# Retention and a squared-ReLU feed-forward on one core: the state's two products in 64-column halves of the array

## The chip, the cores and the metric

One NeuronCore of a Trainium2 chip runs the whole kernel. Its engines are called as in the profile: PE is TensorE (matmuls), PEld its weight loads, DVE is VectorE, ACT is ScalarE, POOL is GpSimd, SP is SyncE, which issues the loads. The metric is the device time of one execution in microseconds (us), lower is better; several executions are timed and their median is given.

## The reference

Retention for 8 sequences of 576 positions and 8 heads of 64, then a feed-forward part over the 4608 tokens that come out (512 wide, 2048 inside):

```python
scores = scale * np.matmul(q, k.transpose(0, 1, 3, 2))
gamma = 1.0 - 2.0 ** (-5.0 - np.arange(H, dtype=np.float32))
Dmat = np.where(rel >= 0, gamma[:, None, None] ** rel[None, :, :], 0.0)   # rel = t - s
x = np.matmul(scores * Dmat[None], v)        # (B, H, S, D), then to (B*S, H*D)
h = np.maximum(x @ w_in, 0.0)
out = (h * h @ w_out).astype(np.float32)
```

q, k, v are float32. The two weights come as float64 and are rounded to float32 on the chip.

## The kernel before

A sequence is taken in chunks of 128 rows, so five of them: four of 128 rows and a last one of 64. With gamma^(t-s) written as gamma^t times gamma^-s, the output of a chunk is q' times a running state U, plus the masked scores of the chunk itself times v', where U is the sum of k^T v' over the chunks before. Heads are taken in pairs, since two heads of 64 fill the 128 partitions; `HP` = 4 is the number of pairs, `hp` counts them, and `e` is 0 or 1 within a pair.

A chunk goes through three functions:

- `turn` (L172) transposes q and k on TensorE (L178) and takes them out of PSUM, q on VectorE with its decay (L181), k on ScalarE (L183).
- `scores` (L185) makes the chunk's own scores (L193). A head's 64 dimensions lie on half of the partitions, so the two heads of a pair use the two row halves of the array. VectorE masks the scores into `ret` (L198) and scales v into `vs` (L202).
- `retain` (L205) makes x of the chunk, transposed, in one PSUM tile `x_ps`, and adds the chunk to U. For each pair the state's product comes first (L212): U of the pair lies in `u_sb` as a 128 x 128 block with one head's 64 x 64 on each end of the diagonal and zeros elsewhere, and one matmul over the whole array serves both heads. Then come the products with the masked scores (L215), one for each head, 64 output columns each, which land on partitions 0 to 63 and 64 to 127: the two column halves of the array. ScalarE copies x to `xT` (L225). U's growth (L231) is one matmul for each pair over the whole array: 128 columns of k against 128 of vs, of which only the two diagonal 64 x 64 blocks are used. ScalarE copies these two blocks of all pairs to the other of two `u_sb` buffers (L237). The first chunk of a sequence has no state's product, the last adds nothing to U.

The form that the profile gives a matmul, such as 128\*64, says how many rows and columns of the array it uses: the contraction by the output's partitions.

The feed-forward part takes blocks of 512 tokens: `ffn_in` (L243) makes 128 of the 2048 inner values for a block with four matmuls (L248), ScalarE applies ReLU (L251), VectorE squares (L253). `ffn_out` (L255) makes a quarter of the sum over the 2048 for 128 tokens with four matmuls (L262); VectorE copies the whole sum out (L266), and POOL's queue stores it (L268).

The order is written out by hand in the loop at L287: step i runs `retain` of chunk i - 2, `scores` of chunk i - 1 and `turn` of chunk i, and after each of the three a third of a chunk's share of feed-forward steps (`ffn`, L276), so that TensorE has work while results leave PSUM. Each step of the feed-forward part also prepares one of 32 pieces of the weights (`prepare`, L132), whose rounding is five operations on VectorE (L122, L127 to L130) and two on POOL (L123, L125), until all are ready. Every engine runs its instructions in the order in which they are written.

Of the kernel before, what the change touches and what calls it, by code (L numbers as in the profile page):

```python
# [9 lines left out]
F32 = mybir.dt.float32  # L10
# [1 line left out]
AF = mybir.ActivationFunctionType  # L12
ALU = mybir.AluOpType

C = 128  # rows of a sequence that are taken at once
TOK = 512  # tokens of a block of the feed-forward part
N_LD = 4  # chunks of q, k and v on chip at once


@with_exitstack  # L20
def kernel(
# [8 lines left out]
    decay_v: bass.AP,  # L30
    out: bass.AP,
):
    """Retention by chunks, with gamma^(t-s) as gamma^t * gamma^-s.

    q is scaled by gamma^t / sqrt(D) where its transpose leaves PSUM, v by gamma^-s, so that

        x[t] = sum_{s <= t} (q'[t] . k[s]) v'[s] = q'[t] U + (the same sum within t's chunk)

    with U = sum k[s]^T v'[s] over the chunks before, which accumulates in PSUM. x comes out
    transposed, as the first product of the feed-forward part takes it, and stays on chip.  # L40

    Everything is in float32. Weights that come in as float64 come as their bits, in int64,
    and are rounded to float32 here.
    """
    nc = tc.nc
    ctx.enter_context(tc.manual_schedule())

    B, H, S, D = q.shape
    HP = H // 2  # pairs of heads: a pair fills the 128 partitions
    d_model = H * D  # L50
    n_tok = B * S
    d_ff = moe_w_in.shape[1]
# [4 lines left out]
    NCH = -(-S // C)  # L57
    chunks = [(b, ci, ci * C, min(C, S - ci * C)) for b in range(B) for ci in range(NCH)]
    N_CH = len(chunks)
    N_PART = 4  # of the sum over d_ff  # L60

    const = ctx.enter_context(tc.tile_pool(name="const", bufs=1))
    ld = ctx.enter_context(tc.tile_pool(name="ld", bufs=N_LD))
    work = ctx.enter_context(tc.tile_pool(name="work", bufs=2))
# [7 lines left out]
    ps_u = ctx.enter_context(tc.tile_pool(name="ps_u", bufs=1, space=PS))  # L72
    ps_f = ctx.enter_context(tc.tile_pool(name="ps_f", bufs=2, space=PS))

    loaded = {}
# [7 lines left out]
            loaded[i].append(t)  # L83

    def w_tile(j):
        """Piece j of the weights: 128 of d_ff, of w_in first."""
        m = j % N_DF
        if j < N_DF:
            t = const.tile([128, N_DM, 128], F32, name=f"w_in{m}")
            src = moe_w_in.rearrange("(c p) f -> p c f", p=128)[:, :, m * 128:(m + 1) * 128]  # L90
        else:
            t = const.tile([128, N_DM, d_model // N_DM], F32, name=f"w_out{m}")
            src = moe_w_out[m * 128:(m + 1) * 128, :].rearrange("p (c f) -> p c f", c=N_DM)
        return t, src
# [13 lines left out]
        raws.append(raw)  # L108

    def round_w(j):  # L110
        """float64 bits to the nearest float32: (mantissa) * 2^(exponent), and the sign.

        What lies under float32's normal numbers becomes 0, what lies over them inf.
        """
        if raws[j] is None:
            return
        words = raws[j].rearrange("p c f -> p (c f)").bitcast(U32).rearrange("p (n two) -> p n two", two=2)
        lo, hi = words[:, :, 0], words[:, :, 1]
        t = w[j].rearrange("p c f -> p (c f)")
        bits = t.bitcast(U32)  # L120
        exp = exp_pool.tile([128, N_DM * 128], U32, tag="exp", name="exp")
        nc.vector.tensor_scalar(exp, hi, 20, 0x7FF, op0=ALU.logical_shift_right, op1=ALU.bitwise_and)  # L122
        nc.gpsimd.tensor_scalar(exp, exp, 1151.0, 896.0, op0=ALU.min, op1=ALU.max)  # L123
        # the bits of 2^(exponent - 1023)
        nc.gpsimd.tensor_scalar(exp, exp, -896.0, 2.0 ** 23, op0=ALU.add, op1=ALU.mult)  # L125
        # the mantissa's upper 21 bits, with the leading 1, and its lower 32 as a fraction
        nc.vector.tensor_scalar(bits, hi, 0xFFFFF, 0x100000, op0=ALU.bitwise_and, op1=ALU.bitwise_or)  # L127
        nc.vector.scalar_tensor_tensor(t, lo, 2.0 ** -32, bits, op0=ALU.mult, op1=ALU.add)
        nc.vector.scalar_tensor_tensor(t, t, 2.0 ** -20, exp.bitcast(F32), op0=ALU.mult, op1=ALU.mult)  # L129
        nc.vector.scalar_tensor_tensor(bits, hi, 0x80000000, bits, op0=ALU.bitwise_and, op1=ALU.bitwise_or)  # L130

    def prepare(last):  # L132
        """The next piece of the weights up to `last`; the loads run two ahead."""
        j = n_ready[0]
        if j > last:
            return
        if j + 2 < 2 * N_DF:
            fetch_w(j + 2)
        round_w(j)
        n_ready[0] += 1  # L140
# [12 lines left out]

    ident = const.tile([128, 128], F32, name="ident")
    make_identity(nc, ident)
    # 1 where t >= s, with s on the partitions
    msk = const.tile([128, 1, C], F32, name="msk")
    nc.gpsimd.memset(msk, 1.0)
    nc.gpsimd.affine_select(
        out=msk[:, 0, :], in_=msk[:, 0, :], compare_op=ALU.is_ge, fill=0.0, base=0,  # L160
        pattern=[[1, C]], channel_multiplier=-1,
    )
    # U of a pair of heads on the diagonal of a 128 x 128 block; the rest stays 0
    u_sb = [const.tile([128, HP, 128], F32, name=f"u_sb{j}") for j in range(2)]
    for t in u_sb:
        nc.gpsimd.memset(t, 0.0)
# [3 lines left out]
    u_ps = [None]  # L170

    def turn(i):  # L172
        """q' and k with the head's dimension on the partitions, two heads to a column block."""
        cs, c0 = chunks[i][3], chunks[i][2]
        for j, name in enumerate(("qT", "kT")):
            p = ps_a.tile([128, HP, C], F32, tag="a", name=f"{name}_ps")
            for hp in range(HP):
                nc.tensor.transpose(p[:, hp, :cs], loaded[i][j][:cs, 2 * hp:2 * hp + 2, :], ident[:cs, :cs])  # L178
            t = st[i][name] = work.tile([128, HP, C], F32, tag=name, name=name)
            if j == 0:  # L180
                nc.vector.tensor_tensor(t[:, :, :cs], p[:, :, :cs], dq[:, :, c0:c0 + cs], op=ALU.mult)  # L181
            else:
                nc.scalar.copy(t[:, :, :cs], p[:, :, :cs])  # L183

    def scores(i):  # L185
        """The chunk's own scores, [s, t], masked; the heads of a pair in banks of their own."""
        b, ci, c0, cs = chunks[i]
        qT, kT = st[i]["qT"], st[i]["kT"]
        sc = [ps_a.tile([128, HP, C], F32, tag="a", name=f"sc{e}") for e in range(2)]
# [13 lines left out]
                                dv[:cs, :, ci:ci + 1].to_broadcast([cs, H, D]), op=ALU.mult)  # L203

    def retain(i):  # L205
        """The chunk's x, transposed, and U with the chunk added."""
        b, ci, c0, cs = chunks[i]
        s = st[i]
        p = ps_a.tile([128, HP, C], F32, tag="a", name="x_ps")
        for hp in range(HP):  # L210
            if ci > 0:
                nc.tensor.matmul(p[:, hp, :cs], lhsT=u_sb[ci % 2][:, hp, :], rhs=s["qT"][:, hp, :cs],  # L212
                                 start=True, stop=False, skip_group_check=True)
            for e in range(2):
                nc.tensor.matmul(p[D * e:D * e + D, hp, :cs], lhsT=s["vs"][:cs, 2 * hp + e, :],  # L215
                                 rhs=s["ret"][e][:cs, hp, :cs], start=(ci == 0), stop=True,
                                 skip_group_check=True)
        tok = b * S + c0
        at = tok
        while at < tok + cs:  # L220
            n = at // TOK
            end = min(tok + cs, (n + 1) * TOK)
            if n not in xT:
                xT[n] = x_pool.tile([128, N_DM, TOK], F32, tag="xT", name="xT")
            nc.scalar.copy(xT[n][:, :, at - n * TOK:end - n * TOK], p[:, :, at - tok:end - tok])  # L225
            at = end
        if ci + 1 < NCH:
            if ci == 0:
                u_ps[0] = ps_u.tile([128, HP, 128], F32, tag="u", name="u_ps")
            for hp in range(HP):  # L230
                nc.tensor.matmul(u_ps[0][:, hp, :], lhsT=loaded[i][1][:cs, 2 * hp:2 * hp + 2, :],  # L231
                                 rhs=s["vs"][:cs, 2 * hp:2 * hp + 2, :], start=(ci == 0 and hp == 0),
                                 stop=(hp == HP - 1), skip_group_check=True)
            u = u_sb[(ci + 1) % 2]
            for e in range(2):
                sl = slice(D * e, D * e + D)
                nc.scalar.copy(u[sl, :, sl], u_ps[0][sl, :, sl])  # L237
        st[i] = loaded[i] = None

    g = {}  # L240
    acc = {}

    def ffn_in(n, m):  # L243
        """relu(x w_in)^2, transposed: 128 of d_ff by a block's tokens."""
        assert m < n_ready[0]
        p = ps_f.tile([128, TOK], F32, tag="h", name="h_ps")
        for cc in range(N_DM):
# [5 lines left out]
        nc.vector.tensor_tensor(g[n, m], r, r, op=ALU.mult)  # L253

    def ffn_out(n, ts, part):  # L255
        """A part of the sum over d_ff for 128 tokens of the block."""
        if part == 0:
            acc[0] = ps_f.tile([128, d_model], F32, tag="o", name="o_ps")
        end = (part + 1) * N_DF // N_PART
# [7 lines left out]
            row = n * TOK + ts * 128  # L267
            nc.gpsimd.dma_start(out[row:row + 128, :], o)  # L268

    # Steps of the feed-forward part stand between those of the retention, so that the tensor  # L270
    # engine has work while results leave PSUM. A block's steps last while as many tokens come in.
    steps = []
    owed = [0.0]
    PER_TOK = (N_DF + N_TS * N_PART) / TOK
# [35 lines left out]


def _decays(B, H, S, D):
    """gamma^t / sqrt(D) by [head's dimension in a pair, pair, t]; gamma^-s by [s in its chunk, head, chunk]."""
    import numpy as np

    gamma = 1.0 - 2.0 ** (-5.0 - np.arange(H))
    t = np.arange(S)
# [38 lines left out]
```

## Time and profile before

| | |
|---|---|
| runs, median | 1265.71 us (1264.05 to 1266.25, three runs) |
| profiled execution, its span | 1263.9 us, 10515 instructions |
| TensorE busy | 1222.0 us, 97% of the span |
| VectorE, ScalarE, POOL busy | 313.0, 154.4, 74.9 us |
| the feed-forward products L248 and L262 | 509.4 and 506.7 us of TensorE's time |
| the retention's products L193, L212, L215, L231 | 44.5, 60.3, 65.0, 39.2 us |
| granted clock of TensorE, mean | 0.986 |

The span runs from the first to the last instruction of the profiled execution; the page shows nothing of that execution outside its span. A group's line gives the source line, engine, operation, tiles and count, then busy time and mean nanoseconds of one, then the idle time of the engine ahead of them and what ended it. A float32 matmul shows as two records with a weight load each, so counts are twice the number of matmuls. Matmuls are pipelined and their ends are modelled, so the mean length of one is much longer than the distance between two; distances between starts are safer.

### The profile page before, as it was taken

What the parts mean: (1) busy time and instruction counts of PE and PEld (TensorE: products, weight loads), DVE (VectorE), ACT (ScalarE), POOL (GpSimd) and SP (SyncE); (2) the same over time, 40 slices, a digit from 0 to 9 for tenths busy, and PEclk for the clock granted to TensorE, in tenths of its full rate; (3) what the DMA queues carried; (4) which work ended last, traced back from release to release, by engine and by line L of the source; (5) the groups of instructions that cost most, each with busy time, mean ns of one, the idle gap of its engine ahead of it and who ended that gap; (6) DMA issues with size and microseconds to landing.
All of it is one profiled execution on the core that took longest, in us unless ns stands there. A gap on an engine that the chain in (4) does not pass through costs nothing.

```text
span 1263.9 us, 10515 instructions
## 1 busy us (share of the span) xinstructions
PE 1222.0 (97%) x4416; PEld 609.8 (48%) x4416; DVE 313.0 (25%) x500; ACT 154.4 (12%) x293; POOL 74.9 (6%) x110
## 2 busy tenths in 40 slices
PE   3698999999999999999999999999999999999998
PEld 2454544544445554445544554454544544444443
DVE  4888811221122112221112112211221122101200
ACT  1111100210012001110121001100210012000100
POOL 2333300000000000000000000000000000000000
PEclk9698999999999999999999999999999999999999
DMA  9655412001210112001110111101121000000000
GB/s 237 180 142 154 117 42 59 5 17 42 59 30 17 33 30 46 21 25 34 42 34 13 34 42 26 42 21 33 25 50 30 26 9 1 9 17 8 1 9 25
DMA packets 126479, 56.41 MB, mean 45 GB/s; under 512 B 113760, under 2 KB 121952, under 8 KB 126304
## 3 DMA queue, kind: packets, MB, share of 16 engines
q1 hardware_dynamic: 123552, 46.30, 15.9%
q0 software_dynamic: 2880, 9.44, 1.9%
q8 instruction: 35, 0.57, 0.2%
q14 instruction: 12, 0.10, 0.0%
HBM read 46.29 MB, written 9.44 MB: 44 GB/s over the span
## 4 chain that ended last, share of the span: by engine, by line
issue 72%; PE 18%; POOL 4%; DVE 4%; SPq 1%; DMA 0%; POOLq 0%
PE o_ps L262 8%; PE h_ps L248 7%; POOL exp L125 1%; POOL out_dram L268 1%; SPq L82 1%; POOL exp L123 1%; PE x_ps L215 1%; DVE w_in L129 1%; DVE w_in L130 1%; PE x_ps L212 1%; PE sc L193 1%; PE u_ps L231 1%; DVE exp L122 1%; DMA raw<-in_moe_w_in_dram 0%; DVE ret L198 0%
## 5 line engine op out<-in xcount | busy, mean ns | idle before, releaser
L248 PE MATMUL h_ps<-xT,w_in 128*128 128x512 f32 x1152 | 509.4, 596 | 0.0
L262 PE MATMUL o_ps<-w_out,g 128*128 128x512 f32 x1152 | 506.7, 594 | 0.0
L248 PEld LDWEIGHTS h_ps<-xT,w_in 128*128 128x128 f32 x1152 | 215.3, 191 | 253.0 <-issue 250.5
L262 PEld LDWEIGHTS o_ps<-w_out,g 128*128 128x128 f32 x1152 | 214.8, 190 | 253.5 <-issue 249.7
L253 DVE TENSOR_TENSOR g<-r 128x512 f32<-128x512 f32 x144 | 99.5, 691 | 405.6 <-ACT r L251 405.6
L251 ACT ACTIVATE r<-h_ps 128x512 f32<-128x512 f32 x144 | 86.0, 597 | 512.4 <-PE h_ps L248 487.5
L198 DVE TENSOR_TENSOR ret<-sc,msk 128x512 f32<-128x512 f32 (+1 forms) x80 | 47.0, 629 | 213.8 <-PE sc L193 213.8
L268 POOL DMA_DIRECT2D out_dram<-o_sb x36 | 19.6, 545 | 1084.0 <-DVE o_sb L266 1084.0
L266 DVE COPY o_sb<-o_ps 128x512 f32<-128x512 f32 x36 | 24.9, 692 | 202.1 <-PE o_ps L262 202.1
L215 PE MATMUL x_ps<-ret,vs 128*64 128x128 f32 (+1 forms) x640 | 65.0, 296 | 0.2 <-DVE vs L202 0.2
L212 PE MATMUL x_ps<-qT,u_sb 128*128 128x128 f32 (+1 forms) x256 | 60.3, 319 | 0.2 <-DVE ret L198 0.2
L212 PEld LDWEIGHTS x_ps<-qT,u_sb 128*128 128x128 f32 x256 | 42.4, 197 | 29.4 <-issue 27.8
L183 ACT COPY kT<-kT_ps 128x512 f32<-128x512 f32 (+1 forms) x40 | 21.7, 543 | 282.7 <-PE kT_ps L178 282.4
L193 PEld LDWEIGHTS sc<-qT,kT 64*128 64x128 f32 (+1 forms) x640 | 37.1, 183 | 32.1 <-issue 30.9
L225 ACT COPY xT<-x_ps 128x512 f32<-128x512 f32 (+1 forms) x44 | 22.0, 509 | 235.2 <-PE x_ps L215 235.2
L178 PE MATMUL kT_ps<-ident,k_ld 128*128 128x128 f32 (+1 forms) x160 | 25.1, 283 | 26.5 <-DVE ret L198 26.4
L181 DVE TENSOR_TENSOR qT<-qT_ps,dq 128x512 f32<-128x512 f32 (+1 forms) x40 | 25.3, 633 | 100.5 <-PE qT_ps L178 90.5
L193 PE MATMUL sc<-qT,kT 64*128 64x128 f32 (+1 forms) x640 | 44.5, 280 | 5.2 <-DVE qT L181 5.2
L215 PEld LDWEIGHTS x_ps<-ret,vs 128*64 128x64 f32 (+1 forms) x640 | 33.8, 141 | 20.7 <-issue 6.9
L231 PE MATMUL u_ps<-vs,k_ld 128*128 128x128 f32 x256 | 39.2, 299 | 0.0
L231 PEld LDWEIGHTS u_ps<-vs,k_ld 128*128 128x128 f32 x256 | 33.0, 201 | 6.0 <-issue 6.0
L178 PEld LDWEIGHTS kT_ps<-ident,k_ld 128*128 128x128 f32 (+1 forms) x160 | 18.8, 149 | 28.2 <-DVE ret L198 27.7
(25 smaller groups left out, 253.3 us busy)
## 6 DMA issues: line engine op xcount, KB each, us to landing
out_dram<-o_sb POOLq DMA_DIRECT2D x36, 256.0 KB, 2.3
q_ld<-in_q_dram SPq DMA_DIRECT2D x32, 256.0 KB, 4.5
k_ld<-in_k_dram SPq DMA_DIRECT2D x32, 256.0 KB, 3.3
v_ld<-in_v_dram SPq DMA_DIRECT2D x32, 256.0 KB, 4.1
raw<-in_moe_w_in_dram SPq DMA_DIRECT2D x16, 512.0 KB, 4.4
raw<-in_moe_w_out_dram SPq DMA_DIRECT2D x16, 512.0 KB, 3.4
dq<-in_decay_q_dram SPq DMA_DIRECT2D x1, 1152.0 KB, 7.1
q_ld<-in_q_dram SPq DMA_DIRECT2D x8, 128.0 KB, 2.9
```

Of the source, the lines that this page charges most:

```text
L178: nc.tensor.transpose(p[:, hp, :cs], loaded[i][j][:cs, 2 * hp:2 * hp + 2, :], ident[:cs, :cs])
L181: nc.vector.tensor_tensor(t[:, :, :cs], p[:, :, :cs], dq[:, :, c0:c0 + cs], op=ALU.mult)
L193: nc.tensor.matmul(sc[e][:cs, hp, :cs], lhsT=kT[sl, hp, :cs], rhs=qT[sl, hp, :cs], start=True, stop=True)
L198: nc.vector.tensor_tensor(r[:cs, :, :cs], sc[e][:cs, :, :cs], msk[:cs, :, :cs].to_broadcast([cs, HP, cs]), op=ALU.mult)
L212: nc.tensor.matmul(p[:, hp, :cs], lhsT=u_sb[ci % 2][:, hp, :], rhs=s["qT"][:, hp, :cs], start=True, stop=False, skip_group_check=True)
L215: nc.tensor.matmul(p[D * e:D * e + D, hp, :cs], lhsT=s["vs"][:cs, 2 * hp + e, :], rhs=s["ret"][e][:cs, hp, :cs], start=(ci == 0), stop=Tru ...
L231: nc.tensor.matmul(u_ps[0][:, hp, :], lhsT=loaded[i][1][:cs, 2 * hp:2 * hp + 2, :], rhs=s["vs"][:cs, 2 * hp:2 * hp + 2, :], start=(ci == 0 ...
L248: nc.tensor.matmul(p, lhsT=w[m][:, cc, :], rhs=xT[n][:, cc, :], start=(cc == 0), stop=(cc == N_DM - 1))
L251: nc.scalar.activation(r, p, AF.Relu)
L253: nc.vector.tensor_tensor(g[n, m], r, r, op=ALU.mult)
L262: nc.tensor.matmul(acc[0], lhsT=g[n, m][:, ts * 128:(ts + 1) * 128], rhs=w[N_DF + m].rearrange("p c f -> p (c f)"), start=(m == 0), stop=( ...
L268: nc.gpsimd.dma_start(out[row:row + 128, :], o)
```

## The change

Both products with the whole array in `retain` are split by head. The state's product becomes two matmuls for a pair, each with 64 columns of `u_sb` and 64 output partitions, and each with the same moving q' (L216 in the new file). U's growth becomes two matmuls for a pair, each with 64 columns of k against 64 of vs (L237 in the new file), and the U tile in PSUM shrinks from 128 to 64 columns for each pair. The flag that starts an accumulation is set only at the first pair of a bank. ScalarE's copy of U keeps its size. The comments and docstrings go too, and lines below move by five or six (the masked scores' product is L220, the feed-forward products are L254 and L268).

```diff
         for hp in range(HP):
             if ci > 0:
-                nc.tensor.matmul(p[:, hp, :cs], lhsT=u_sb[ci % 2][:, hp, :], rhs=s["qT"][:, hp, :cs],
-                                 start=True, stop=False, skip_group_check=True)
+                for e in range(2):
+                    half = slice(D * e, D * e + D)
+                    nc.tensor.matmul(p[half, hp, :cs], lhsT=u_sb[ci % 2][:, hp, half], rhs=s["qT"][:, hp, :cs],
+                                     start=(hp == 0), stop=False, skip_group_check=True)
             for e in range(2):
-                nc.tensor.matmul(p[D * e:D * e + D, hp, :cs], lhsT=s["vs"][:cs, 2 * hp + e, :],
-                                 rhs=s["ret"][e][:cs, hp, :cs], start=(ci == 0), stop=True,
+                half = slice(D * e, D * e + D)
+                nc.tensor.matmul(p[half, hp, :cs], lhsT=s["vs"][:cs, 2 * hp + e, :],
+                                 rhs=s["ret"][e][:cs, hp, :cs], start=(ci == 0 and hp == 0), stop=True,
                                  skip_group_check=True)
...
-                u_ps[0] = ps_u.tile([128, HP, 128], F32, tag="u", name="u_ps")
+                u_ps[0] = ps_u.tile([128, HP, D], F32, tag="u", name="u_ps")
             for hp in range(HP):
-                nc.tensor.matmul(u_ps[0][:, hp, :], lhsT=loaded[i][1][:cs, 2 * hp:2 * hp + 2, :],
-                                 rhs=s["vs"][:cs, 2 * hp:2 * hp + 2, :], start=(ci == 0 and hp == 0),
-                                 stop=(hp == HP - 1), skip_group_check=True)
+                for e in range(2):
+                    nc.tensor.matmul(u_ps[0][D * e:D * e + D, hp, :], lhsT=loaded[i][1][:cs, 2 * hp + e, :],
+                                     rhs=s["vs"][:cs, 2 * hp + e, :], start=(ci == 0 and hp == 0),
+                                     stop=(hp == HP - 1), skip_group_check=True)
             u = u_sb[(ci + 1) % 2]
             for e in range(2):
-                sl = slice(D * e, D * e + D)
-                nc.scalar.copy(u[sl, :, sl], u_ps[0][sl, :, sl])
+                half = slice(D * e, D * e + D)
+                nc.scalar.copy(u[half, :, half], u_ps[0][half, :, :])
```

On TensorE, the second chunk of the second sequence: the end of the feed-forward steps, the last of its four pairs of heads (the three before it read the same), U and the next feed-forward product. Sizes are output partitions by columns, and the numbers behind a name are its buffer. Before:

```order
L262 MATMUL o_ps<-w_out_616,g 128x512
...
L212 MATMUL x_ps<-qT,u_sb_133 128x128
L215 MATMUL x_ps<-ret_860,vs 64x128
L215 MATMUL x_ps<-ret_862,vs 64x128
L231 MATMUL u_ps<-vs,k_ld 128x128 x4
L262 MATMUL o_ps<-w_out_636,g 128x512
```

And the same place with the change:

```order
L268 MATMUL o_ps<-w_out_644,g 128x512
...
L216 MATMUL x_ps<-qT,u_sb_133 64x128 x2
L220 MATMUL x_ps<-ret_896,vs 64x128
L220 MATMUL x_ps<-ret_898,vs 64x128
L237 MATMUL u_ps<-vs,k_ld 64x64 x8
L268 MATMUL o_ps<-w_out_664,g 128x512
```

Each product over the whole array has become two over 64 output partitions, at the same place; nothing else changed places, and every other engine runs the same instructions as before.

In a sequence's last chunk of 64 rows, before and then with the change (here the masked scores' products contract over 64 rows, the state's over 128; the other pairs read the same):

```order
L248 MATMUL h_ps<-xT,w_in_202 128x512 x4
L212 MATMUL x_ps<-qT,u_sb_132 128x64
L215 MATMUL x_ps<-ret_525,vs 64x64
L215 MATMUL x_ps<-ret_527,vs 64x64
...
L248 MATMUL h_ps<-xT,w_in_237 128x512 x4
```

```order
L254 MATMUL h_ps<-xT,w_in_202 128x512 x4
L216 MATMUL x_ps<-qT,u_sb_132 64x64 x2
L220 MATMUL x_ps<-ret_553,vs 64x64
L220 MATMUL x_ps<-ret_555,vs 64x64
...
L254 MATMUL h_ps<-xT,w_in_241 128x512 x4
```

The state's product became two matmuls here too, between the same neighbours.

## Prediction

> **What bounds the kernel now.** The page comes first: its busy line, and the groups of TensorE (PE).
>
> ```profile
> PE 1222.0 (97%) x4416; PEld 609.8 (48%) x4416; DVE 313.0 (25%) x500; ACT 154.4 (12%) x293; POOL 74.9 (6%) x110
> L248 PE MATMUL h_ps<-xT,w_in 128*128 128x512 f32 x1152 | 509.4, 596 | 0.0
> L262 PE MATMUL o_ps<-w_out,g 128*128 128x512 f32 x1152 | 506.7, 594 | 0.0
> ```
>
> TensorE works 97% of the span, and 1016 of its 1222 us are the two feed-forward products, which the change leaves alone. Every float32 matmul leaves two records: L248 runs 576 matmuls and shows 1152. Next come the waits, TensorE's over the whole span and VectorE's (DVE) from 20 to 157 us, and the busy time after 160 us with its granted clock (the last but two figures: 1.00).
>
> ```profile
> PE kT_ps L178 <- DVE ret L198: 26.4, 5, 6.9
> PE sc L193 <- DVE qT L181: 5.2, 2, 4.4
> 104.08 1.12 PE L178 MATMUL kT_ps<-ident,k_ld 128*128 128x128 f32 x4 [5.92 <-DVE ret L198]
> DVE w_out L129 <- POOL exp L125: 8.2, 16, 0.5
> DVE w_in L129 <- POOL exp L125: 7.7, 15, 0.5
> DVE exp L122 <- DMA raw<-in_moe_w_in_dram: 0.8, 1, 0.8
> 160.00:1264.00 1104.00, 1098.28 (x3868) 538.59 (x3866) 187.53 (x292) 130.88 (x249) 19.63 (x36) 1.00 0.11 27
> ```
>
> There are two stages. Until 104 us VectorE sets the pace, with the rounding of the weights: TensorE waits for it, and VectorE itself waits for POOL and once for a load, never for TensorE. From 104 us on TensorE waits for nothing, and whatever shortens its stream shortens the kernel. So I price the change on TensorE alone, from the timeline of TensorE, where a row is start, length, line, operation and number of records. A row's length includes a modelled tail, so I use differences of starts. A middle chunk (128 rows, with a state before it and after it):
>
> ```profile
> 617.51 0.38 PE L212 MATMUL x_ps<-qT,u_sb 128*128 128x128 f32 x2
> 617.82 0.44 PE L215 MATMUL x_ps<-ret,vs 128*64 128x128 f32 x4
> 618.19 0.49 PE L212 MATMUL x_ps<-qT,u_sb 128*128 128x128 f32 x2
> ...
> 620.55 1.16 PE L231 MATMUL u_ps<-vs,k_ld 128*128 128x128 f32 x8
> 621.55 7.03 PE L248 MATMUL h_ps<-xT,w_in 128*128 128x512 f32 x16
> ```
>
> The form K*M says which part of the array is used: 128*128 is all of it, 128*64 a column half. x takes 620.55 - 617.51 = 3.04 us and U 1.00, together 4.04. Then the first chunk of a sequence, which has no state to multiply with, and a last chunk of 64 rows, which adds nothing to U:
>
> ```profile
> 394.56 7.03 PE L248 MATMUL h_ps<-xT,w_in 128*128 128x512 f32 x16
> 401.52 1.09 PE L215 MATMUL x_ps<-ret,vs 128*64 128x128 f32 x16
> 402.54 1.16 PE L231 MATMUL u_ps<-vs,k_ld 128*128 128x128 f32 x8
> 403.54 7.03 PE L248 MATMUL h_ps<-xT,w_in 128*128 128x512 f32 x16
> ...
> 360.83 0.68 PE L193 MATMUL sc<-qT,kT 64*64 64x64 f32 x16
> 361.44 10.57 PE L248 MATMUL h_ps<-xT,w_in 128*128 128x512 f32 x24
> ...
> 372.72 10.47 PE L248 MATMUL h_ps<-xT,w_in 128*128 128x512 f32 x24
> 383.02 0.33 PE L212 MATMUL x_ps<-qT,u_sb 128*128 128x64 f32 x2
> 383.28 0.33 PE L215 MATMUL x_ps<-ret,vs 64*64 64x64 f32 x4
> 383.54 0.43 PE L212 MATMUL x_ps<-qT,u_sb 128*128 128x64 f32 x2
> ...
> 385.42 3.70 PE L248 MATMUL h_ps<-xT,w_in 128*128 128x512 f32 x8
> ```
>
> The first chunk takes 1.02 + 1.00 = 2.02 us, the last 385.42 - 383.02 = 2.40.
>
> **What a record and a change of tile cost.** Sixteen records of column halves in one stream take 1.02 us to the start of what follows; four between full-array products take 618.19 - 617.82 = 0.37. The difference is 0.65 us for 12 records: 0.054 us a record with 128 moving columns, so a pair of halves (0.108) costs hardly more than one. [...] With 64 moving columns, 16 records (L193, row halves) take 361.44 - 360.83 = 0.61 us and four (L215, column halves) 383.54 - 383.28 = 0.26: 0.029 a record and 0.14 per stretch. That mixes row with column halves; it is the nearest that the trace has. At the edges: 16 feed-forward records ahead of the column halves take 401.52 - 394.56 = 6.96 us, while 24 ahead of L212 take 383.02 - 372.72 = 10.30, that is 6.87 for 16. Entering the halves thus costs 0.09 us more. And the feed-forward products behind halves run longer (10.57 against 10.47), as their first load lies open: 0.10.
>
> **The change, part by part.** x of a middle chunk: L212's 8 records become 16 of column halves, so all 32 are one stretch and seven of its eight changes of tile are gone. 32 x 0.054 = 1.73 us. U: 8 records of 125 ns become 16 with 64 moving columns, in the same tile shape, with no change between x and U: 16 x 0.029 = 0.47. One stretch 0.15, entering 0.09, leaving 0.10. Sum 2.54 against 4.04: 1.50 us saved. First chunk: x stays, U gains, the change between them goes; 16 x 0.054 + 0.47 + 0.15 + 0.10 = 1.59 against 2.02 (entering is paid today too): 0.43 saved.
>
> Last chunk: the masked product contracts over 64 rows and the state's product over 128, so its tiles are 64*64 and 128*64 in turn, and I keep an emptied array between them: 8 groups of 0.26 are 2.08, with entering 2.17, against 2.40: 0.23 saved. The trace has no change from 128*64 to 64*64. If none were paid, 32 x 0.029 + 0.15 + 0.09 = 1.17 would save 1.23. The row decides for the first: 128*128 to 64*64 costs the 0.14 today. [...]
>
> How many chunks count: 8 sequences of five chunks.
>
> ```profile
> L212 PE MATMUL x_ps<-qT,u_sb 128*128 128x128 f32 x192 | 47.2, 330 | 0.2 <-DVE ret L198 0.2
> L212 PE MATMUL x_ps<-qT,u_sb 128*128 128x64 f32 x64 | 13.1, 286 | 0.0
> L231 PE MATMUL u_ps<-vs,k_ld 128*128 128x128 f32 x256 | 39.2, 299 | 0.0
> ```
>
> At 8 records each these are 24 middle chunks, 8 last ones and 32 that add to U (24 + 8 first). The first sequence's five lie before 104 us, where VectorE is the cover: what TensorE saves there it waits longer. Seven sequences are left: 21 x 1.50 + 7 x 0.43 + 7 x 0.23 = 31.5 + 3.0 + 1.6 = 36.1 us.
>
> Is VectorE late next? It rounds until 157.6 us, and TensorE has by then gained 0.43 + 1.50 = 1.9 us on it.
>
> ```profile
> 156.94 0.69 DVE L130 SCALAR_TENSOR_TENSOR w_out<-raw,w_out 128x512 uint32<-128x512 uint32 x1
> 157.69 10.57 PE L262 MATMUL o_ps<-w_out,g 128*128 128x512 f32 x24
> ```
>
> That last piece (ready at 156.94 + 0.69 = 157.63) is read by the fourth matmul of the L262 group, its seventh record, at 157.69 + 6 x 0.43 = 160.3 now and at 158.4 then, still after. I take the 1.9 us as kept; lost, they bring the gain to 34.2. ScalarE's (ACT) copies keep their sizes, half of the U bank was never copied, and no wait or DMA is added or moved, so every other queue costs nothing.
>
> The profiled execution's span is 1263.9 us, so I expect a span of 1227.8. The page shows no time around the span; the median of the runs is 1265.71, 1.8 more, which I carry over: 1265.7 - 36.1 = 1229.6 us.
>
> **The rivals.** First: 64 moving columns cost in U what 128 do. For it: no row shows column halves with K = 128 and 64 columns in a stream. Against it: L193 runs 16 such records in 0.61. Price: 16 x (0.054 - 0.029) = 0.40 us in 28 chunks, 11.2; time 1240.8.
>
> Second: the change doesn't do what it says, because both halves of the state's product stream the same qT, and take turns. L215's halves, which do run together, have different moving tiles, so the trace is silent. Price: 16 records at twice the time, 0.86 us in 21 chunks and 16 x 0.029 = 0.46 in 7, together 21.3; time 1250.9.
>
> Third: weight loads come into the open, as a load for one column half can't run under a matmul in the other.
>
> ```profile
> L212 PEld LDWEIGHTS x_ps<-qT,u_sb x256: 186/189/338, 34.5 to 1127.0; 128*128 128x128 f32 x128
> 618.19 0.30 PEld L212 LDWEIGHTS x_ps<-qT,u_sb 128*128 128x128 f32 x2 [0.17 <-issue]
> ```
>
> A load of 128 columns lasts 0.30 - 0.189 = 0.11 us from start to start where it lies open, so 64 columns 0.055. At 24 open pairs in a middle chunk and U's 8 in a first, 21 x 1.32 + 7 x 0.44 = 30.8 us are lost; time 1260.4. Against it: L215's stream, where a pair takes 0.108 us with its loads. [...]
>
> Fourth, slower: the array is emptied not for a new tile shape but at each new group of operands, so that every four records keep the 0.15. L216 and L220 alternate, and each group of L220 adds to sums that L216 just wrote. x then takes 8 x 0.37 = 2.96, U 4 x (4 x 0.029 + 0.15) = 1.07, with the edges 4.22 against 4.04 in a middle chunk; a first one 1.02 + 1.07 + 0.10 = 2.19 against 2.02; the last as forecast. 21 x 0.18 + 7 x 0.17 - 1.6 = 3.4 us slower; time 1269.1. It decides from 36.1 / (21 x 11 + 7 x 4) = 0.14 us per group on. Against it: in L215's 16 records the operands change seven times for nothing.
>
> **How the numbers follow.** The forecast has 0.78, with 1222.6 (no change of tile paid in the last chunks, 7 x 1.00 more) to 1231.5 (the 1.9 us lost) as its own bounds. The rivals in their order have 0.08, 0.05, 0.04 and 0.03; 0.02 is left for a gain that something hides wholly. The range takes in the forecast and the first rival, 0.86: 1222 to 1241. About 0.2%, 2.5 us, is what a measurement can tell from no change, and the three runs spread over 2.2. All cases but the fourth and the last remainder are faster by more: 0.95 faster, 0.02 the same, 0.03 slower.
>
> **What would show it.** In the profile after, a middle chunk should last 1.73 + 0.47 + 0.15 = 2.35 us from its first L216 to the next feed-forward record; U's row of 16 records should be about 0.7 long; rows of L216 and L220 should follow each other by about 0.22 us in a middle chunk and by about 0.26 in the last; TensorE should wait longer for ret before 104 us and for nothing after it; the granted clock after 160 us should stay 1.00. If U's records start 0.054 us apart, the first rival is right; if L216's four records take 0.43, the second; if pairs take 0.16, the third; if groups follow by 0.37, the fourth. A wait of L262 for w_out near 158 us would show the 1.9 us lost.

## The result, and the profile after

The median went from 1265.98 us (four runs, 1264.05 to 1266.72) to 1228.91 (four runs, 1228.20 to 1230.46): a ratio of 0.9708, 95% interval 0.9694 to 0.9722, 37.1 us less. The profiled execution took 1230.46 us with a span of 1228.7, so 1.8 us lay around the span here too; the forecast span was 1227.8. The two spans differ by 35.2 us.

The page after, in its busy line and the groups that answer to those shown of before, and the window after 160 us, whose granted clock (the last but two figures) is 1.00 as before:

```profile
PE 1180.5 (96%) x4928; PEld 588.9 (48%) x4928; DVE 313.0 (25%) x500; ACT 151.4 (12%) x293; POOL 74.8 (6%) x110
L254 PE MATMUL h_ps<-xT,w_in 128*128 128x512 f32 x1152 | 511.5, 598 | 1.3 <-ACT r L257 1.3
L268 PE MATMUL o_ps<-w_out,g 128*128 128x512 f32 x1152 | 508.2, 596 | 0.0
160.00:1228.00 1068.00, 1063.13 (x4289) 519.38 (x4287) 187.61 (x292) 128.19 (x249) 19.60 (x36) 1.00 0.12 28
```

TensorE has 512 records more and is busy for 41.5 us less; VectorE's work is the same to a tenth. The feed-forward products grew by 3.6 us. Most of it lies behind U, where 16 of their records now make a row of 7.13 us in place of 7.03, in 28 places. The timeline of TensorE, a middle chunk of the same sequence as before:

```profile
600.88 0.44 PE L216 MATMUL x_ps<-qT,u_sb 128*64 128x128 f32 x4
601.15 0.39 PE L220 MATMUL x_ps<-ret,vs 128*64 128x128 f32 x4
601.37 0.39 PE L216 MATMUL x_ps<-qT,u_sb 128*64 128x128 f32 x4
...
602.46 0.39 PE L220 MATMUL x_ps<-ret,vs 128*64 128x128 f32 x4
602.68 0.63 PE L237 MATMUL u_ps<-vs,k_ld 128*64 128x64 f32 x16
603.25 7.13 PE L254 MATMUL h_ps<-xT,w_in 128*128 128x512 f32 x16
```

From the first L216 to the feed-forward product are 603.25 - 600.88 = 2.37 us, where 4.04 stood and 2.35 was forecast. Groups of four follow each other by 0.22 (601.37 - 601.15) for L216 and L220 alike, and the 16 records of U take 0.57. A last chunk and the first one of the next sequence:

```profile
373.60 0.34 PE L216 MATMUL x_ps<-qT,u_sb 128*64 128x64 f32 x4
373.87 0.33 PE L220 MATMUL x_ps<-ret,vs 64*64 64x64 f32 x4
374.13 0.34 PE L216 MATMUL x_ps<-qT,u_sb 128*64 128x64 f32 x4
...
375.71 3.70 PE L254 MATMUL h_ps<-xT,w_in 128*128 128x512 f32 x8
...
391.80 1.09 PE L220 MATMUL x_ps<-ret,vs 128*64 128x128 f32 x16
392.73 0.64 PE L237 MATMUL u_ps<-vs,k_ld 128*64 128x64 f32 x16
393.29 7.13 PE L254 MATMUL h_ps<-xT,w_in 128*128 128x512 f32 x16
```

The last chunk takes 2.11 us (2.08 forecast, 2.40 before), and its groups follow by 0.26: the alternation of 64\*64 and 128\*64 is paid. The first takes 1.49 (2.02 before).

The waits of TensorE, up to 105 us; from there to the end the same view has no row at all:

```profile
PE kT_ps L178 <- DVE ret L198: 30.2, 5, 7.0
PE sc L193 <- DVE qT L181: 6.3, 2, 4.9
PE qT_ps L178 <- DMA q_ld<-in_q_dram: 4.2, 1, 4.2
PE h_ps L254 <- ACT r L257: 1.3, 1, 1.3
PE sc L193 <- ACT xT L230: 0.3, 1, 0.3
...
104.13 1.11 PE L178 MATMUL kT_ps<-ident,k_ld 128*128 128x128 f32 x4 [6.99 <-DVE ret L198]
```

The wait for `ret` has grown from 26.4 to 30.2 us and that for `qT` from 5.2 to 6.3, and TensorE's last wait ends at 104.13 us (the last line, from its timeline) where it ended at 104.08: the first sequence's saving went into waiting. The two waits for ScalarE are new, 1.6 us together, though the prediction held that no wait is added. They too lie in the stage that VectorE sets and cost nothing.

### The profile page after: what moved, and what is told of

Same layout as the page of the kernel before. It is cut to its first block, busy times and chain, and to the rows that moved or that the text cites. A ratio compares the mean times of both kernels' runs of the same rounds, so it can differ in the third digit from the quotient of the medians.

```text
span 1228.7 us, 11538 instructions
## 1 busy us (share of the span) xinstructions
PE 1180.5 (96%) x4928; PEld 588.9 (48%) x4928; DVE 313.0 (25%) x500; ACT 151.4 (12%) x293; POOL 74.8 (6%) x110
## 4 chain that ended last, share of the span: by engine, by line
issue 72%; PE 18%; POOL 4%; DVE 4%; SPq 2%; DMA 0%; POOLq 0%
PE o_ps L268 8%; PE h_ps L254 7%; POOL exp L125 1%; SPq L82 1%; POOL out_dram L274 1%; POOL exp L123 1%; DVE w_in L129 1%; DVE w_in L130 1%; PE sc L193 1%; PE x_ps L220 1%; DVE exp L122 1%; PE x_ps L216 1%; DMA raw<-in_moe_w_in_dram 0%; DVE ret L198 0%; PE kT_ps L178 0%
## 5 line engine op out<-in xcount | busy, mean ns | idle before, releaser
L254 PE MATMUL h_ps<-xT,w_in 128*128 128x512 f32 x1152 | 511.5, 598 | 1.3 <-ACT r L257 1.3
L268 PE MATMUL o_ps<-w_out,g 128*128 128x512 f32 x1152 | 508.2, 596 | 0.0
L254 PEld LDWEIGHTS h_ps<-xT,w_in 128*128 128x128 f32 x1152 | 215.3, 191 | 256.0 <-issue 250.4
L268 PEld LDWEIGHTS o_ps<-w_out,g 128*128 128x128 f32 x1152 | 214.7, 190 | 254.5 <-issue 249.7
L220 PE MATMUL x_ps<-ret,vs 128*64 128x128 f32 (+1 forms) x640 | 60.6, 283 | 0.2 <-DVE vs L202 0.2
L178 PE MATMUL kT_ps<-ident,k_ld 128*128 128x128 f32 (+1 forms) x160 | 25.3, 285 | 30.2 <-DVE ret L198 30.2
L216 PE MATMUL x_ps<-qT,u_sb 128*64 128x128 f32 (+1 forms) x512 | 52.3, 284 | 0.0
L220 PEld LDWEIGHTS x_ps<-ret,vs 128*64 128x64 f32 (+1 forms) x640 | 40.3, 145 | 8.2 <-issue 5.3
L216 PEld LDWEIGHTS x_ps<-qT,u_sb 128*64 128x64 f32 x512 | 31.4, 144 | 24.4 <-issue 21.3
L178 PEld LDWEIGHTS qT_ps<-ident,q_ld 128*128 128x128 f32 (+1 forms) x160 | 19.2, 146 | 24.8 <-issue 24.7
L125 POOL TENSOR_SCALAR exp<-exp 128x512 uint32<-128x512 uint32 x32 | 30.0, 936 | 2.6
```

The costliest lines, as they stand in the source:

```text
L216: nc.tensor.matmul(p[half, hp, :cs], lhsT=u_sb[ci % 2][:, hp, half], rhs=s["qT"][:, hp, :cs], start=(hp == 0), stop=False, skip_group_chec ...
L220: nc.tensor.matmul(p[half, hp, :cs], lhsT=s["vs"][:cs, 2 * hp + e, :], rhs=s["ret"][e][:cs, hp, :cs], start=(ci == 0 and hp == 0), stop=Tr ...
L254: nc.tensor.matmul(p, lhsT=w[m][:, cc, :], rhs=xT[n][:, cc, :], start=(cc == 0), stop=(cc == N_DM - 1))
L268: nc.tensor.matmul(acc[0], lhsT=g[n, m][:, ts * 128:(ts + 1) * 128], rhs=w[N_DF + m].rearrange("p c f -> p (c f)"), start=(m == 0), stop=( ...
```

## The experiments

The theory: changes of tile shape cost 0.15 to 0.20 us each, and U's whole product streams twice the columns that it needs. The rivals are named with each run. The kernel before was run again beside them, on the same chip: its median was 1265.5 us with the first four runs and 1265.6 with the last two. Times of two changed kernels are compared by their medians.

**One half of the change, then the other.** First the state's product alone:

```diff
             if ci > 0:
-                nc.tensor.matmul(p[:, hp, :cs], lhsT=u_sb[ci % 2][:, hp, :], rhs=s["qT"][:, hp, :cs],
-                                 start=True, stop=False, skip_group_check=True)
+                for e in range(2):
+                    half = slice(D * e, D * e + D)
+                    nc.tensor.matmul(p[half, hp, :cs], lhsT=u_sb[ci % 2][:, hp, half], rhs=s["qT"][:, hp, :cs],
+                                     start=(hp == 0), stop=False, skip_group_check=True)
...
```

> The kernel before with the state's product split into column halves, and U's growth left as one product over the whole array. Theory (the gain is made of changes of tile shape that are gone, and of U's halved columns): a middle chunk takes 1.73 + 0.15 for x and 1.00 for U, with 0.09 for entering 2.97 us against 4.04; a last chunk saves 0.23, a first one nothing. 21 x 1.07 + 7 x 0.23 = 24.1 us: 1241.8. Rival (x and U gain only together, because the array must stay in one shape from the first product to the last): well under 24 us.

Measured: 1240.48 us, ratio 0.9807 (0.9792 to 0.9822), 25.0 us less. Then U alone:

```diff
-                u_ps[0] = ps_u.tile([128, HP, 128], F32, tag="u", name="u_ps")
+                u_ps[0] = ps_u.tile([128, HP, D], F32, tag="u", name="u_ps")
...
-                nc.tensor.matmul(u_ps[0][:, hp, :], lhsT=loaded[i][1][:cs, 2 * hp:2 * hp + 2, :],
-                                 rhs=s["vs"][:cs, 2 * hp:2 * hp + 2, :], start=(ci == 0 and hp == 0),
+                for e in range(2):
+                    nc.tensor.matmul(u_ps[0][D * e:D * e + D, hp, :], lhsT=loaded[i][1][:cs, 2 * hp + e, :],
+                                     rhs=s["vs"][:cs, 2 * hp + e, :], start=(ci == 0 and hp == 0),
...
```

> The kernel before with U's growth alone split into column halves. Theory: x keeps its eight changes of shape but the last of them moves behind U; 2.89 + 0.47 + 0.15 + 0.10 = 3.61 us in a middle chunk against 4.04, and 0.43 in a first one as well: 28 x 0.43 = 12.0 us: 1253.9. With the run that splits the state's product alone it should add up to the whole gain of 37 us within 2. Rival (only together): the two sum to much less than 37.

Measured: 1253.54 us, ratio 0.9904 (0.9889 to 0.9919), 12.0 us less. The two sum to 37.0, against 37.1 for both: they add up within the 2 us expected, and closer than the spread of the runs can tell, and the rival falls. The timeline of the run with U alone, at the end of a middle chunk, shows how:

```profile
579.80 0.49 PE L212 MATMUL x_ps<-qT,u_sb 128*128 128x128 f32 x2
580.22 0.44 PE L215 MATMUL x_ps<-ret,vs 128*64 128x128 f32 x4
580.49 0.63 PE L232 MATMUL u_ps<-vs,k_ld 128*64 128x64 f32 x16
581.06 7.13 PE L263 MATMUL o_ps<-w_out,g 128*128 128x512 f32 x16
```

The last L215 of a chunk is followed after 0.27 us instead of 0.37, since U has its shape, and U takes 0.57.

**Nothing split, only the order.** The state's products of all pairs over the whole array come first, then all masked products:

```diff
-        for hp in range(HP):
-            if ci > 0:
+        if ci > 0:
+            for hp in range(HP):
                 nc.tensor.matmul(p[:, hp, :cs], lhsT=u_sb[ci % 2][:, hp, :], rhs=s["qT"][:, hp, :cs],
-                                 start=True, stop=False, skip_group_check=True)
+                                 start=(hp == 0), stop=False, skip_group_check=True)
+        for hp in range(HP):
             for e in range(2):
...
```

> The kernel before, nothing split: the state's products of all four pairs over the whole array first, then all masked products in halves, so that x has one change of shape where it had seven between its products. Theory (changes of shape cost 0.15 to 0.20 us each, and a halved state's product needs as long for its columns, 4 x 0.054, as a whole one, 2 x 0.11): a middle chunk takes 8 x 0.11 + 0.09 + 1.02 + 1.00 = 3.0 us against 4.04, a last one 0.26 + 6 x 0.11 + 16 x 0.029 + 0.15 = 1.5 against 2.40; 21 x 1.04 + 7 x 0.9 = 28 us: 1237.6, faster than splitting the state's product alone. Rival (the gain comes from the halves running side by side, as the change's name says): little from the order alone, 1260 or more.

Measured: 1238.33 us, ratio 0.9782 (0.9768 to 0.9797), 27.2 us less. A middle chunk of its timeline:

```profile
605.89 1.05 PE L212 MATMUL x_ps<-qT,u_sb 128*128 128x128 f32 x8
606.88 1.09 PE L216 MATMUL x_ps<-ret,vs 128*64 128x128 f32 x16
607.90 1.16 PE L232 MATMUL u_ps<-vs,k_ld 128*128 128x128 f32 x8
608.90 7.03 PE L249 MATMUL h_ps<-xT,w_in 128*128 128x512 f32 x16
```

x takes 607.90 - 605.89 = 2.01 us with whole products in a row, where it took 3.04, and the whole chunk 3.01. Three trips from the whole array into the halves and back are gone. By the prediction's terms (entering 0.09, one stretch 0.15, leaving 0.10) a trip costs 0.34 us and three cost 1.02; x lost 1.03. The start flags changed with the order and were not tried alone, but this price was taken from rows of before and leaves nothing over for them.

So the order alone gives more than splitting the state's product alone (27.2 against 25.0 us; the two intervals overlap slightly, but each of its four runs is faster than each of the other's). Its advantage lies in the last chunks, which still alternate when split (2.11 us, as in the changed kernel) and don't when grouped. They take 378.82 - 377.28 = 1.54 us here:

```profile
377.28 1.00 PE L212 MATMUL x_ps<-qT,u_sb 128*128 128x64 f32 x8
378.21 0.68 PE L216 MATMUL x_ps<-ret,vs 64*64 64x64 f32 x16
378.82 3.70 PE L249 MATMUL h_ps<-xT,w_in 128*128 128x512 f32 x8
```

In a middle chunk halves side by side are hardly faster than the whole array: eight whole records take 0.99 us (606.88 - 605.89), sixteen halves in the grouped run below 0.93 (341.39 - 340.46). What was saved there is the change of shape between products, and the rival, that the gain comes from the halves running at once, falls. With the 64 moving columns of a last chunk it is otherwise: eight whole records take 0.93 us (378.21 - 377.28), hardly less than with 128 columns, and sixteen halves 0.61 (372.79 - 372.18 in the grouped run).

**U's halves with 128 moving columns.** On the changed kernel; U's tile in PSUM is 128 columns wide again, and half of what the halves make isn't used:

```diff
...
-                                     rhs=s["vs"][:cs, 2 * hp + e, :], start=(ci == 0 and hp == 0),
+                                     rhs=s["vs"][:cs, 2 * hp:2 * hp + 2, :], start=(ci == 0 and hp == 0),
...
```

> The changed kernel with U's halves streaming 128 columns of v' again, of which only 64 are used. Theory: 16 records of 0.054 in place of 0.035 or less (0.029 in the forecast): 0.40 us in 28 chunks, 11 us slower than the changed kernel: 1240. Rival (records of 64 columns are bound by their weight loads or by issue, not by their columns): no difference, 1229.

Measured: 1241.72 us, ratio to before 0.9809 (0.9792 to 0.9825): 12.8 us above the changed kernel's median, 11.4 in the spans (1240.1 against 1228.7). U in its timeline, in a first chunk:

```profile
395.89 1.04 PE L237 MATMUL u_ps<-vs,k_ld 128*64 128x128 f32 x16
396.86 7.13 PE L254 MATMUL h_ps<-xT,w_in 128*128 128x512 f32 x16
```

It takes 0.97 us instead of 0.56 in the same place of the changed kernel, 0.41 more where 0.40 was computed. For U's halves the theory's other half holds: the gain is the halved columns. Halves of 128 columns need 0.97 where the whole product needed 1.00, and had it stayed so, the change would have brought 24 us. The wider tile is not the cause: in the run with the first sequence alone, halves of 64 columns write into a tile of that size, and their row is 0.63 us long as in the changed kernel. Fewer columns without the split are not shown to help: by the last chunk above, whole records of 64 columns took nearly as long as those of 128.

**Halves, grouped.** The changed kernel with the state's products of all pairs ahead of the masked ones:

```diff
-        for hp in range(HP):
-            if ci > 0:
+        if ci > 0:
+            for hp in range(HP):
                 for e in range(2):
...
+        for hp in range(HP):
             for e in range(2):
```

> The changed kernel with the state's products of all four pairs ahead of all masked products. In a middle chunk all are of one shape and nothing should change; in a last chunk the eight alternating groups (128*64 and 64*64) become two stretches. Theory (any change of the tile's shape empties the array, a change of its rows too): 0.09 + 2 x (16 x 0.029 + 0.15) = 1.32 us against 2.11 + 0.09, in 7 chunks: 6.2 us below the changed kernel, 1222.7. Rival (the 0.26 us of a group in a last chunk is not a change of shape but the price of a short group): 1229.

Measured: 1223.41 us, ratio to before 0.9662 (0.9649 to 0.9675): 5.5 us below the changed kernel, whose interval begins at 0.9694, above the end of this one. Its timeline, a middle chunk and then a last chunk:

```profile
340.46 1.09 PE L216 MATMUL x_ps<-qT,u_sb 128*64 128x128 f32 x16
341.39 1.04 PE L221 MATMUL x_ps<-ret,vs 128*64 128x128 f32 x16
342.26 0.64 PE L238 MATMUL u_ps<-vs,k_ld 128*64 128x64 f32 x16
342.83 7.13 PE L255 MATMUL h_ps<-xT,w_in 128*128 128x512 f32 x16
...
372.18 0.69 PE L216 MATMUL x_ps<-qT,u_sb 128*64 128x64 f32 x16
372.79 0.68 PE L221 MATMUL x_ps<-ret,vs 64*64 64x64 f32 x16
373.40 3.70 PE L255 MATMUL h_ps<-xT,w_in 128*128 128x512 f32 x8
```

The last chunk takes 1.22 us instead of 2.11, twice 0.61, and a middle one 2.37 (342.83 - 340.46) as in the changed kernel. Six changes are gone from the last chunk, at (2.11 - 1.22) / 6 = 0.15 us each: a change of the tile's rows alone (128\*64 to 64\*64) is paid like one from the whole array. The rival falls: in a middle chunk of the changed kernel, groups of four follow each other by 0.22 us, their 4 x 0.054 and nothing more, though they are as short and each L220 adds to sums that L216 just wrote. This is the fastest version of the study, and it differs from the changed kernel by the order of two loops.

**The first sequence alone.** Both splits where `b == 0`, with U's halves in the first 64 columns of a U tile of the old size, and the kernel before elsewhere:

```diff
+        if b == 0:
+            for hp in range(HP):
+                if ci > 0:
+                    for e in range(2):
...
+        else:
+            for hp in range(HP):
+                if ci > 0:
+                    nc.tensor.matmul(p[:, hp, :cs], lhsT=u_sb[ci % 2][:, hp, :], rhs=s["qT"][:, hp, :cs],
...
```

> The kernel before with both splits for the first of the eight sequences alone. Theory (VectorE sets the pace there and never waits for TensorE): no gain, 1265.7, at most 1 us to either side. Rival (a share of what TensorE saves there reaches the end): up to 0.43 + 3 x 1.50 + 0.23 = 5.2 us, 1260.5.

Measured: 1266.17 us, ratio 1.0001 (0.9992 to 1.0010), over 11 runs and 15 of before. 5.2 us would have been a ratio of 0.996; the rival falls. The waits of TensorE over its whole run, and VectorE's from 20 to 157 us:

```profile
PE kT_ps L178 <- DVE ret L198: 32.1, 5, 7.0
PE sc L193 <- DVE qT L181: 8.7, 4, 5.3
```

```profile
DVE w_out L129 <- POOL exp L125: 7.7, 15, 0.5
DVE w_in L129 <- POOL exp L125: 7.7, 15, 0.5
DVE exp L122 <- DMA raw<-in_moe_w_in_dram: 0.8, 1, 0.8
```

TensorE waits 32.1 us for `ret` instead of 26.4, and VectorE never waits for TensorE in this stretch.

## Why the prediction was right

The forecast was 1229.6 us and the measured median 1228.91; the gain was forecast at 36.1 and came out at 37.1 by the medians and 35.2 by the profiled spans. Runs of one kernel lie over 2 us apart, so a miss of 0.7 us is smaller than they can tell, and in that a matter of luck; the terms of the sum are the better test.

- **A stage set by VectorE, one by TensorE.** Right, by the run with the first sequence alone, and by TensorE's empty list of waits after 105 us.
- **Middle chunk.** 2.35 us forecast, 2.37 found (2.36 in others). The 0.054 us of a record held for L216, whose two halves stream the same q': the second rival falls. The 0.029 of a U record held (16 in 0.57 us, 0.47 and the 0.10 or so of the change behind them): the first falls.
- **Changes of tile.** Priced at 0.15 a stretch from the difference of two rows (0.37 - 4 x 0.054), with 0.09 and 0.10 at its edges, and shown by reordering: whole products in a row, without any split, gave 27.2 us. That the array is emptied in the 0.15 us was the author's assumption, and no run shows it. The runs show the time, and where the weight loads start: in the trace of before, the first load behind halves starts with its matmul (both at 361.44 us), behind transposes over the whole array 0.11 us ahead of it (372.61 and 372.72). The fourth rival, which has the 0.15 paid at each new group of operands, falls with groups 0.22 apart in place of 0.37.
- **Weight loads.** The 16 pairs of x in a middle chunk stay at 0.11 us a pair, loads included (602.68 - 600.88 = 1.80 us for all), and so do U's eight pairs in the run that gives them 128 columns (0.97 for all, with the change behind them), so the third rival falls: with loads in the open a pair would have taken 0.16. In that middle chunk the load records of a group start 0.10 to 0.11 us ahead of its matmuls (601.05 and 601.15 us for the first L220), within the row of the group before (600.88 to 601.32).
- **Last chunk.** Here the trace had no row, and the choice was between 0.23 and 1.23 us saved. Found: 2.40 - 2.11 = 0.29, less the 0.09 for entering, 0.20. The row of 0.14 decided rightly, and the grouped halves (1.22 us) agree: a change of rows costs 0.15 us too.
- **VectorE late next.** The 1.9 us were kept: TensorE is 0.64 us behind its old time at the second sequence's first `retain` (114.58 against 113.94) and 1.28 ahead at the group that ends the first sum (156.41 against 157.69). With the change, VectorE's timeline has the last piece of weights and the mask behind it without a gap:

```profile
156.97 0.69 DVE L130 SCALAR_TENSOR_TENSOR w_out<-raw,w_out 128x512 uint32<-128x512 uint32 x1
157.58 1.28 DVE L198 TENSOR_TENSOR ret<-sc,msk 128x512 f32<-128x512 f32 x2
```

Before, VectorE waited 0.15 us for the scores there; now they are ready earlier. The seventh record of TensorE's group needs the piece at about 156.41 + 6 x 0.43 = 159.0, and it is ready at 157.66.

- **The span.** 0.9 us longer than forecast, of which 0.6 lie ahead of the second sequence: its first `retain` starts at 114.58 us where it started at 113.94. From there to the end the span is 1149.96 us before and 1114.12 after, 35.8 less; the chunks as found, with the prediction's edges, give 21 x 1.48 + 7 x 0.43 + 7 x 0.20 = 35.5.

## What to carry to other kernels

Before splitting or merging small matmuls, look at how the tile's shape alternates in TensorE's order: in this kernel a change cost 0.15 to 0.17 us (0.89 for six in a last chunk, 1.03 for six in a middle one), about as much as three records of 128 columns in halves, and putting products of one shape in a row gave 27.2 us, most of the gain, without splitting anything. Splitting paid by itself where it let half the columns go, as in U. Where the zeros lay in the stationary operand and 128 moving columns stayed, two halves took nearly as long as one whole; with 64 moving columns they were faster (0.61 against 0.93 us), for whole records hardly got shorter there. A stage's price can be had from the difference of a long and a short stretch of the same records in the trace of before, and only chunks in the stage that TensorE sets may be counted.

## What the runs showed of the hardware that was not expected

TensorE came back slowly from a wait, and not equally slowly each time. After the wait for `ret` that ends at 103 to 105 us, the next 16 feed-forward records (6.9 us elsewhere) took 8.2 to 9.5 us from start to start in the eight profiles. The two rows are of the changed kernel, then of the grouped halves, each with the window from 108 to 110 us:

```profile
105.04 9.61 PE L254 MATMUL h_ps<-xT,w_in 128*128 128x512 f32 x16
114.58 1.09 PE L220 MATMUL x_ps<-ret,vs 128*64 128x128 f32 x16
108.00:110.00 2.00, 2.00 (x3) 0.67 (x2) 1.97 (x4) 0.00 (x0) 0.00 (x0) 0.50 0.03 4
```

```profile
105.74 8.27 PE L255 MATMUL h_ps<-xT,w_in 128*128 128x512 f32 x16
113.95 1.09 PE L221 MATMUL x_ps<-ret,vs 128*64 128x128 f32 x16
108.00:110.00 2.00, 2.00 (x6) 0.77 (x5) 1.79 (x3) 0.00 (x0) 0.14 (x1) 0.94 0.00 0
```

They took 9.5 and 8.2 us from start to start. From 104 to 108 us the granted clock was 0.50 in the first, as in the profile of before; from 108 to 110 it was still 0.50 in the first and 0.94 in the second. In the profile of before it was 0.75 there; a quarter of the clock over 2 us makes 0.5 of the 0.6 us by which the changed kernel began its second sequence later. Whether this is also why runs of one kernel lie 2 us apart is not shown: each kernel has one profile, and the four runs of the changed kernel took 1230.46, 1228.96, 1228.87 and 1228.20 us at mean clocks of 0.980, 0.988, 0.986 and 0.983. What sets the moment at which the clock returns was not tried.
